# Routed experts 1 to 7 in 64-token tiles of plain 32-bit floats

## The chip, the core and the metric

The kernel runs on one core of a Trainium2 chip. The core has a matrix engine (TensorE, PE in the profile), two engines for elementwise work (VectorE, DVE; ScalarE, ACT), GpSimd (POOL), which here only issues indirect DMAs, and SyncE (SP), which issues the other DMAs. The metric is the device time of one execution in microseconds; a lower time is better.

## The reference

Three stages, all in 32-bit floats. Attention over a window of 128 positions, a dense layer with squared ReLU, and eight routed experts; the change lies in the third.

```python
x = attention(q, k, v)                      # 4 x 8 heads x 576 x 64 -> 2304 tokens x 512
r = maximum(x @ w_in, 0); x = (s * r * r + b) @ w_out          # 512 -> 2048 -> 512
out = x.copy()
do_compute = x @ w_skip > 0;  xc = x[do_compute]
logits = xc @ w_gate;  e_idx = argmax(logits);  gate_w = softmax(logits)[e_idx]
for e in range(8):
    mask = e_idx == e
    h = maximum(xc[mask] @ w1[e], 0.0)                         # 512 -> 1024
    y[mask] = gate_w[mask, None] * (h @ w2[e])                 # 1024 -> 512
out[do_compute] = xc + y
```

For the input given, the routing sends 639, 194, 63, 83, 51, 20, 167 and 143 tokens to experts 0 to 7; 944 tokens of the 2304 skip.

## The kernel before

Tokens are worked on in six blocks of 384 (NB). Attention of a later block is woven between the dense layer's products of an earlier one. Matrix products are made in a fast 32-bit form of PE (F32R) whose inputs are split in a high and a low part (tiles wh and wl, xh and xl): three products, high by high, high by low, low by high, stand for one. The attention's own products (scores s_ps, line 132, and PV o_ps, lines 223 and 253) and all transposes use plain 32-bit floats, unsplit. The PV products of a pair of heads have 64 output columns each and write two halves of PSUM's partitions.

The routing (`route`) of each block writes the numbers of an expert's tokens to a list in DRAM (`lst`), and the dense layer's result goes to DRAM (`x2d`, and `out` for the tokens that skip). In the last block (j = NB - 1) one weight piece of the experts per step m is split (`split`): an expert's weights are 8 pieces of 128 x 1024 (512 KB), each split by one ACT copy (L617) and one DVE subtraction (L68) into wh and wl. Raw pieces arrive in a ring of 5 places, later 12 (`pump`, `Stream`).

`moe2` works through the experts in tiles of 128 tokens. A tile is gathered by an indirect DMA of POOL (xg, L741) by the list in `la`; transposed by PE into p_x (L747) and split into xth and xtl; multiplied with w1 (`gemm1`, 24 products of 512 columns, L755); the ReLU'd result is transposed (`h_t`, 8 transposes, L778) and split; multiplied with w2 (`gemm2`, 24 products, L765); weighted and added by DVE (`fin`, L769) and scattered by POOL (L772). One `step` holds the first products of tile t, the second products of tile t - 1, and between the two halves of these the transposes of tile t + 1. The number of tiles of an expert is known only at run time: `chain` is a tree of branches, one per tile, and `hint` tells PE ahead which way the next one goes. Within the experts ACT, DVE and POOL run in the order in which the code is written; PE's and SP's order, and all that stands ahead of it, is a scheduler's.

```python
            step((e, k), e, prev2, 8 * e + 12, k % 2, 2 if e == 0 else 0, (e, k + 1))
            chain(e, k + 1, e)
```

The lines of these functions as the profile numbers them:

Of the kernel before, what the change touches and what calls it, by code (L numbers as in the profile page):

```python
# [25 lines left out]
KMAX = 6  # L26
BIG = 1 << 20
LE = 128 * 32
RING, MORE = 5, 7
# [4 lines left out]
def body(tc, q_in, k_in, vl, wm, we, wg, wgt, s_in, b_in, mask_in, cst_in, rout_in, ids_in, out):  # L34
# [613 lines left out]
    for j in range(NB):  # L648
        if j:
            split_x(j)  # L650
        if j == NB - 1:
            ast.close()
            R = mk("moe2", ast, side="right", reuse_waits="tile")
            ws.free.extend(R.tile([128, 1024], F32, name=f"ring{i}") for i in range(RING))
            pump()
            later = moe2(tc, locals_ns(locals())).send
# [7 lines left out]
        for m in range(NM):  # L664
# [35 lines left out]
class Stream:  # L700


    def __init__(self):
        self.loaded, self.split, self.places, self.free, self.at = 0, 0, RING, [], {}

    def state(self):
        return self.loaded, self.split, self.places, list(self.free), dict(self.at)

    def back_to(self, st):
        self.loaded, self.split, self.places, self.free, self.at = *st[:3], list(st[3]), dict(st[4])  # L710


# [5 lines left out]
def moe2(tc, L):  # L718
    nc = tc.nc
    main, psum, lst, x2d, out = L.main, L.psum, L.lst, L.x2d, L.out  # L720
    cnt, rc, ident, eh, el, split, ws = L.cnt, L.rc, L.ident, L.eh, L.el, L.split, L.ws
    C = L.R
    xg = [C.tile([128, DM], F32, name=f"xg{i}") for i in range(3)]
    lt = [C.tile([128, 2], U32, name=f"lt{i}") for i in range(3)]
    ls = [C.tile([128, 2], U32, name=f"ls{i}") for i in range(4)]
    la = C.tile([128, NE, NTILE, 2], U32, name="la")
# [7 lines left out]
    extra = []  # L734
    bank = lambda tag, name, bufs=1: psum.tile([128, 512], F32, name=name, tag=tag, bufs=bufs)

    def gather(e, k, rows=NT):
        if (e, k) != (0, 1):
            nc.vector.tensor_copy(lt[0], la[:, e, k, :])
        idx = la[:, e, k, 0:1] if isinstance(k, int) and (e, k) != (0, 1) else lt[0][:, 0:1]  # L740
        nc.gpsimd.indirect_dma_start(  # L741
            out=xg[0], out_offset=None, in_=x2d[0:rows], in_offset=bass.IndirectOffsetOnAxis(ap=idx, axis=0),
            bounds_check=rows - 1, oob_is_err=False)

    def x_t():
        for k in range(4):
            nc.tensor.transpose(p_x[:, k * 128:(k + 1) * 128], xg[0][:, k * 128:(k + 1) * 128], ident)  # L747
# [20 lines left out]
    def fin(n):  # L768
        nc.vector.scalar_tensor_tensor(out=og, in0=p_o, scalar=lt[2][:, 1:2].bitcast(F32), in1=xg[2],  # L769
                                       op0=ALU.mult, op1=ALU.add)  # L770
        nc.vector.tensor_copy(ls[n], lt[2])
        nc.gpsimd.indirect_dma_start(  # L772
            out=out, out_offset=bass.IndirectOffsetOnAxis(ap=ls[n][:, 0:1], axis=0), in_=og, in_offset=None,
            bounds_check=NT - 1, oob_is_err=False)
# [207 lines left out]
```

## Time and profile before

| | us |
|---|---|
| median of 3 timed runs | 802.49 (799.76 to 802.6) |
| profiled execution | 804.8 |
| its span, first to last instruction | 803.0 |
| expert 1's first tile begins on PE (in the span) | 646.98 |
| last second product ends | about 795.6 |

The profile's page gives busy time per engine and 40 equal slices of the span (each 20 us; a digit is tenths). Other views give busy time in chosen stretches, the instructions in order of time (a row may stand for several like ones: the count stands behind the x, the time is from the first's start to the last's end), and for a tile how long its DMAs took from issue to landing. A PE record's end is modelled, so records overlap; what an operation costs PE is the distance between starts. "128*64 128x128" is a product with 128 contraction rows, 64 output columns of the stationary operand, and a moving operand of 128 columns.

### The profile page before, as it was taken

The page shows a single profiled execution, that of the slowest core. Times are in us where ns is not written, and L with a number is a line of the kernel's source. Part 1 is how long each engine was busy: PE and PEld are TensorE (multiplying, and loading weights), DVE is VectorE, ACT ScalarE, POOL GpSimd, SP SyncE. Part 2 cuts the span into 40 slices and gives each one's busy share as a digit, 9 for nine tenths or more (in the row PEclk, how much of TensorE's full clock was granted, in tenths as well). Part 3 has the DMA queues.
Part 4 walks back from the last instruction along what each step waited for, and adds up shares of the span by engine and source line. Part 5 has one row for each costly group of instructions (what it writes and reads, how often), then busy time and mean ns, then how long its engine had stood idle before and what let it go on. Part 6 is the DMA issues. An engine that isn't in the chain of part 4 may idle for free.

```text
span 803.0 us, 12461 instructions
## 1 busy us (share of the span) xinstructions
PE 748.8 (93%) x4166; PEld 614.1 (76%) x4166; DVE 542.5 (68%) x1655; ACT 374.4 (47%) x871; POOL 52.9 (7%) x56
## 2 busy tenths in 40 slices
PE   7889889989999999979999999999999999878996
PEld 4568767768788888868888888989877877666784
DVE  5889999885358954686547972699642264878651
ACT  4656555534455444535555332545522245557440
POOL 0000000000010001000001010000121111111110
PEclk9879999999999999999999999999999999999999
DMA  8945341532105310432112250354443341877100
GB/s 247 319 152 186 119 155 36 181 99 67 54 17 162 89 37 24 145 103 71 35 47 101 79 171 1 124 167 142 135 149 131 133 142 66 307 254 285 38 23 15
DMA packets 50609, 96.53 MB, mean 120 GB/s; under 512 B 8555, under 2 KB 25963, under 8 KB 50497
## 3 DMA queue, kind: packets, MB, share of 16 engines
q1 hardware_dynamic: 45600, 85.82, 33.6%
q0 software_dynamic: 2976, 5.59, 2.2%
q10 hardware_dynamic: 1920, 3.80, 1.4%
q8 instruction: 49, 0.80, 0.4%
q14 instruction: 64, 0.52, 0.2%
HBM read 83.83 MB, written 13.65 MB: 121 GB/s over the span
## 4 chain that ended last, share of the span: by engine, by line
PE 56%; DMA 16%; DVE 15%; issue 8%; ACT 2%; SPq 1%; another core or an unknown queue 0%; POOL 0%; POOLq 0%; DVEq 0%; ACTq 0%
PE acc L126 20%; PE h_ps L126 20%; DMA out<-og,ls 8%; DMA xg<-x2d,la 5%; PE s_ps L126 3%; PE o_ps L126 3%; PE t_ps L126 3%; DVE wl L68 3%; PE p_o L765 2%; DMA hp<-wgt 2%; DVE hp L373 2%; DVE hp L375 2%; PE p_h L755 2%; DVE tp L168 1%; DVE tp L155 1%
## 5 line engine op out<-in xcount | busy, mean ns | idle before, releaser
L126 PE MATMUL h_ps<-xh,wh 128*128 128x384 f32 x380 | 133.9, 352 | 1.3 <-ACT wh L378 1.3
L126 PE MATMUL h_ps<-xh,wl 128*128 128x384 f32 x380 | 129.5, 341 | 3.4 <-DVE wl L68 3.4
L126 PE MATMUL h_ps<-xl,wh 128*128 128x384 f32 x380 | 128.8, 339 | 0.0
L436 ACT ACTIVATE r<-h_ps 128x384 f32<-128x384 f32 x96 | 47.0, 490 | 113.1 <-PE h_ps L126 87.5
L497 DVE CUSTOM_DVE_ANT_0 junk<-x,hp 128x512 bf16<-128x512 f32 x135 | 92.6, 686 | 9.3 <-DMA hp<-wgt 7.8
L437 DVE SCALAR_TENSOR_TENSOR r<-r,sb 128x384 f32<-128x384 f32 x96 | 58.9, 614 | 57.4 <-ACT r L436 57.1
L163 ACT ACTIVATE tp<-tp,stat 128x256 f32<-128x256 f32 (+2 forms) x160 | 74.6, 468 | 41.3 <-DVE stat L155 40.8
L126 PE MATMUL acc<-wh,gh 128*128 128x512 f32 x288 | 86.9, 409 | 0.7 <-ACT gh L446 0.7
L126 PE MATMUL acc<-wh,gl 128*128 128x512 f32 x288 | 84.1, 400 | 0.1
L126 PE MATMUL acc<-wl,gh 128*128 128x512 f32 x288 | 83.0, 396 | 0.0
L446 ACT ACTIVATE gh<-r,sb 128x384 fp32r<-128x384 f32 x96 | 59.2, 617 | 47.0 <-DVE r L437 46.5
L126 PEld LDWEIGHTS h_ps<-xh,wh 128*128 128x128 f32 x380 | 72.1, 190 | 10.4 <-issue 3.8
L155 DVE CUSTOM_DVE_ANT_0 tp<-s_ps,masks 128x256 f32<-128x256 f32 (+2 forms) x160 | 52.6, 378 | 35.1 <-PE s_ps L126 27.2
L126 PEld LDWEIGHTS h_ps<-xh,wl 128*128 128x128 f32 x380 | 72.0, 190 | 5.4 <-DVE wl L68 5.3
L447 DVE SCALAR_TENSOR_TENSOR gl<-r,sb,gh 128x384 fp32r<-128x384 f32 x96 | 59.1, 616 | 22.4 <-ACT gh L446 21.7
L126 PEld LDWEIGHTS h_ps<-xl,wh 128*128 128x128 f32 x380 | 72.2, 190 | 2.0
L126 PEld LDWEIGHTS acc<-wh,gl 128*128 128x128 f32 x288 | 54.2, 190 | 14.6 <-DVE gl L447 1.9
L126 PEld LDWEIGHTS acc<-wl,gh 128*128 128x128 f32 x288 | 54.4, 189 | 12.7
L126 PEld LDWEIGHTS acc<-wh,gh 128*128 128x128 f32 x288 | 50.1, 189 | 10.2 <-issue 3.4
L755 PE MATMUL p_h<-wh,xth 128*128 128x512 f32 x120 | 49.5, 412 | 6.7 <-ACT wh L617 4.4
L591 POOL DMA_INDIRECT lst<-pay,di x18 | 18.9, 1049 | 538.4 <-DVE di L589 534.5
L126 PE MATMUL t_ps<-cst,tp 128*128 128x128 f32 (+1 forms) x246 | 37.2, 271 | 14.5 <-DVE tp L168 13.1
(131 smaller groups left out, 1275.4 us busy)
## 6 DMA issues: line engine op xcount, KB each, us to landing
ring<-we SPq DMA_DIRECT2D x36, 512.0 KB, 4.1
w_words<-wm SPq DMA_DIRECT2D x30, 512.0 KB, 4.7
hp<-wgt SPq DMA_DIRECT2D x45, 256.0 KB, 3.2
more<-we SPq DMA_DIRECT2D x21, 512.0 KB, 5.5
vt<-vl SPq DMA_DIRECT2D x32, 192.0 KB, 2.6
x2d<-x SPq DMA_DIRECT2D x17, 256.0 KB, 2.6
out<-x SPq DMA_DIRECT2D x17, 256.0 KB, 3.0
more<-we ACTq DMA_DIRECT2D x7, 512.0 KB, 3.5
```

The costliest lines, as they stand in the source:

```text
L68: nc.vector.tensor_tensor(out=out_, in0=x, in1=hi.bitcast(F32), op=ALU.subtract)
L126: i = f(*args, **kw)
L155: anchor['v'] = nc.vector.tensor_tensor_reduce(out=t[0:nr, i, c0:c0 + n], in0=ps[i][0:nr, c0:c0 + n], in1=masks[0:nr, 2 * units[u][1] + i, ...
L163: anchor['s'] = nc.scalar.activation(out=t[0:nr, i, c0:c0 + n], in_=t[0:nr, i, c0:c0 + n], func=ACTF.Exp, scale=-1.0, bias=st[0:nr, 0, i:i ...
L373: nc.vector.scalar_tensor_tensor(out=bits, in0=hi, scalar=0xC0000000, in1=bits, op0=ALU.bitwise_and, op1=ALU.bitwise_or)
L436: nc.scalar.activation(out=r, in_=hp, func=ACTF.Relu)
L437: nc.vector.scalar_tensor_tensor(out=r, in0=r, scalar=sb[:, 0:1], in1=r, op0=ALU.mult, op1=ALU.mult)
L446: nc.scalar.activation(out=gh, in_=r, func=ACTF.Identity, bias=sb[:, 1:2])
L447: nc.vector.scalar_tensor_tensor(out=gl, in0=r, scalar=sb[:, 1:2], in1=gh.bitcast(F32), op0=ALU.add, op1=ALU.subtract)
L497: nc.vector.tensor_tensor_reduce(out=junk, in0=x2t[j, t], in1=w, scale=1.0, scalar=0.0, op0=ALU.mult, op1=ALU.add, accum_out=lgs[j][:, t, ...
L591: i = nc.gpsimd.indirect_dma_start(out=lst, out_offset=bass.IndirectOffsetOnAxis(ap=di[:, t:t + 1], axis=0), in_=pay[:, t, :], in_offset=N ...
L755: nc.tensor.matmul(p_h[f], lhsT=x[:, k * 128:(k + 1) * 128], rhs=w[:, f * 512:(f + 1) * 512], start=n == 0, stop=n == 11)
```

## The change

Expert 0 keeps its tiles of 128, its split weights and its steps (`step0`, `chain0`, `leave0`). For experts 1 to 7:

- A tile has 64 tokens. A token's row of 512 is two rows of 256 (`x2h`), so a gather brings 128 half rows: the first halves of 64 tokens on partitions 0 to 63, the second halves on 64 to 127. The list is kept in that layout (`l2`, four loads, then a shift and an or by DVE).
- Products are in plain 32-bit floats, with unsplit weights. The 64 tokens are the stationary operand; the output columns are split in two halves, which go to PSUM partitions 0 to 63 and 64 to 127 (`tile_position`). Per tile 8 calls of 512 columns, 16 calls of 256, and 6 transposes.
- Raw weights lie in 42 places: 3 of the ring, 16 that held split weights 8 to 15 of the dense layer (one pair free after each step of the last block), 7 of the pool `more`, 16 that held expert 0's split weights. The last 14 of the 56 pieces reuse places of expert 1 and what follows.
- The gather of a tile is issued one step earlier than before, into one of four buffers of half the width.
- The last dense block splits 8 pieces, not 16.

```diff
+NQ = 2
+TT = 128 // NQ
+TMAX = 6
 BIG = 1 << 20
 LE = 128 * 32
-RING, MORE = 5, 7
+RING, MORE = 3, 7
+NP = 16 + RING + MORE + 16
...
-    eh, el = {}, {}
-    ws = Stream()
-
-    def pump(eng=nc.sync):
-        while ws.free and ws.loaded < 8 * NE:
-            t, i = divmod(ws.loaded, 8)
-            ws.at[ws.loaded] = ws.free.pop(0)
-            eng.dma_start(out=ws.at[ws.loaded], in_=we[t, i])
-            ws.loaded += 1
-
-    def split(t, i):
-        n = 8 * t + i
-        p = t % 2
-        if (p, i) not in eh:
-            eh[p, i] = W(8 * p + i, "wh")
-            el[p, i] = W(8 * p + i, "wl")
-        raw = ws.at.pop(n)
-        nc.scalar.copy(eh[p, i], raw)
-        lower(el[p, i], raw, eh[p, i])
-        ws.free.append(raw)
-        ws.split = n + 1
-        pump()
...
+    eh, el, raws, pools = {}, {}, {}, {}
+
+    def at_place(n):
+        if n >= NP:
+            return raws[n - NP]
+        if n < RING:
+            return pools["ring"].tile([128, 1024], F32, name=f"ring{n}", tag=f"ring{n}")
+        n -= RING
+        if n < 16:
+            name = f"{('wh', 'wl')[n % 2]}{8 + n // 2}"
+            return main.tile([128, 1024], F32, name="raw", tag=name)
+        n -= 16
+        if n < MORE:
+            return pools["more"].tile([128, 1024], F32, name=f"more{n}", tag=f"more{n}")
+        n -= MORE
+        return main.tile([128, 1024], F32, name="raw", tag=f"{('wh', 'wl')[n % 2]}{n // 2}")
+
+    def fetch(a, b):
+
+        for n in range(a, min(b, 8 * (NE - 1))):
+            raws[n] = at_place(n)
+            nc.sync.dma_start(out=raws[n], in_=we[1 + n // 8, n % 8])
...
+    def fetch0(i):
+
+        if i < 8:
+            spl[i] = pools["ring"].tile([128, 1024], F32, name=f"ring{i % RING}", tag=f"ring{i % RING}")
+            nc.sync.dma_start(out=spl[i], in_=we[0, i])
+
+    def split(i):
+        raw = spl.pop(i)
+        eh[0, i], el[0, i] = W(i, "wh"), W(i, "wl")
+        nc.scalar.copy(eh[0, i], raw)
+        lower(el[0, i], raw, eh[0, i])
...
-            if j == NB - 1:
-                split(*divmod(m, 8))
+            if j == NB - 1 and m < 8:
+                split(m)
+                fetch0(m + RING)
+            elif j == NB - 1:
+
+                if m == 8:
+                    fetch(0, RING)
+                else:
+                    fetch(RING + 2 * (m - 9), RING + 2 * (m - 8))
     last = g2(NB - 1, NM - 1)
+    fetch(RING + 14, RING + 16)
...
+    x2h = x2d.rearrange("n (h d) -> (n h) d", h=NQ)
+    outh = out.rearrange("n (h d) -> (n h) d", h=NQ)
+    xt, ht = xf[0:2]
...
+    def step0(at, second):
+
+
+        if second:
+            shift(1)
+        shift(0)
+        if at is not None:
+            nc.vector.tensor_copy(lf[0], la[:, at, :])
+            rows(xf[0], x2d, lf[0][:, 0:1], NT)
+        gemm1(0, 0)
+        gemm1(0, 1)
+        if second:
+            gemm2(0, 0)
+            if at is not None:
+                x_t(xf[0])
...
+    def leave0():
+        step0(None, True)
+        shift(1)
+        sx_t(here(1, 0))
+        gemm2(0, 0)
+        gemm2(0, 1)
+        fin(3)
+        fetch(NP - 16, NP)
...
+    def sx_t(x):
+        for k in range(XK):
+            nc.tensor.transpose(p_x[:, k * 128:(k + 1) * 128], x[:, k * 128:(k + 1) * 128], ident)
+        nc.vector.tensor_copy(xt[:, 0:HD], p_x[:, 0:HD])
+
+    def sgemm1(e):
+        for k in range(4):
+            for f in range(NQ):
+                nc.tensor.matmul(p_h[0][TT * f:TT * f + TT, 0:HF], lhsT=xt[:, part(k, XK)],
+                                 rhs=w(e, k)[:, f * HF:(f + 1) * HF], start=k == 0, stop=k == 3,
+                                 tile_position=(0, TT * f))
+        nc.scalar.activation(out=r[:, 0:HF], in_=p_h[0][:, 0:HF], func=ACTF.Relu)
+
+    def sgemm2(e, cs):
+        for c in cs:
+            o = (c % 2) * 512
+            for f in range(NQ):
+                nc.tensor.matmul(p_o[TT * f:TT * f + TT, 0:HD], lhsT=ht[:, part(c, HK)],
+                                 rhs=w(e, 4 + c // 2)[:, o + f * HD:o + (f + 1) * HD], start=c == 0, stop=c == 7,
+                                 tile_position=(0, TT * f))
...
+    def sh_t():
+        for c in range(HK):
+            nc.tensor.transpose(p_t[0][:, c * 128:(c + 1) * 128], r[:, c * 128:(c + 1) * 128], ident)
+        nc.scalar.copy(ht[:, 0:HF], p_t[0][:, 0:HF])
...
+    def step(x, cur, e1, e2, n=0, then=None, pre=(), new=None):
+
+
         if e2 is not None:
...
+            second()
+        nc.vector.tensor_copy(xg[0][:, 0:HD], cur[0])
+        nc.vector.tensor_copy(xg[0][:, HD:HD + 2].bitcast(U32), cur[1])
...
+        for p in pre:
+            gather(*p)
+        sgemm1(e1)
+        if then:
+            hint(*then)
+        if e2 is not None:
+            sgemm2(e2, range(4))
+        if x is not None:
+            sx_t(x)
+        if e2 is not None:
+            sgemm2(e2, range(4, 8))
+            sfin(n)
+        sh_t()
...
+            pre = [(e + 1, 1)] + ([(e + 2, 0)] if e + 2 < NE else [])
+            step(here(e + 1, 0), cur, e, prev2, 2 + e % 2, (e + 1, 1), pre)
+            if e > 1:
+                fetch(NP + 8 * (e - 2), NP + 8 * (e - 1))
...
+        fetch(NP - 16 - MORE, NP - 16)
...
-        step((0, 1), None, None, 16)
-        nc.scalar.dma_start(out=la[:, 1:NE], in_=lv[:, 1:NE, 0:NTILE])
-        _, K = nc.values_load_multi_w_load_instructions(ki[0:1, :], min_val=0, max_val=NTILE - 1)
-        K = [k + 1 for k in K]
+        x_t(xf[0])
+        for i in range(NQ):
+            for q in range(NQ):
+                nc.scalar.dma_start(out=l2[TT * q:TT * q + TT, :, i], in_=lv[TT * i:TT * i + TT, 1:NE, 0:NTILE])
...
+            for q in range(NQ):
+                s = slice(TT * q, TT * q + TT)
+                nc.vector.tensor_scalar(out=l2[s, :, :, :, 0], in0=l2[s, :, :, :, 0], scalar1=NQ // 2, scalar2=q,
+                                        op0=ALU.logical_shift_left, op1=ALU.bitwise_or)
+            for p in ((1, 0), (1, 1), (2, 0)):
+                gather(*p)
+
+            step0(2, False)
+            chain0(3)
+            leave0()
+            for e in range(1, NE):
+                chain(e, 1, e - 1 if e > 1 else None, (here(e, 0), meta(e, 0)))
```

On POOL, at the start of the experts (`xg` and `xf` hold a 128-token tile of expert 0, `xn` the 64-token tiles of experts 1 to 7, `ki` the tile counts, `l` the list `l2`), before:

```order
L741 DMA xg_6019<-x2d,lt_6022 128x512
L591 DMA lst<-pay,di 32768x2 x3
L772 DMA out<-og,ls_6026 2304x512
L909 TENSOR_LOAD ki
L852 REGISTER_ALU
L852 COMPARE_AND_BRANCH
L741 DMA xg_6019<-x2d,la 128x512
```

and now:

```order
L774 DMA xf_6017<-x2d,lf_6020 128x512
L596 DMA lst<-pay,di 32768x2 x3
L779 DMA out<-og,ls_6028 2304x512
L1040 TENSOR_LOAD ki
L1041 TENSOR_LOAD ki
L774 DMA xn<-x2d,l_6032 128x256 x3
L774 DMA xf_6017<-x2d,lf_6020 128x512
```

Three gathers for experts 1 and 2 now stand ahead of the gather of expert 0's third tile.

On SP, the same place (`la` is the list of expert 0, `more` are weight places), before:

```order
L475 DMA x2d<-x_6246 128x512
L476 DMA out<-x_6246 128x512
L909 TENSOR_LOAD ki
L909 ISA x16
L901 DMA la<-lst 128x32
L852 REGISTER_ALU
L852 COMPARE_AND_BRANCH
```

and now:

```order
L1041 ISA x10
L1028 DMA la<-lst 128x32
L628 DMA more_6444<-we 128x1024
L628 DMA more_6446<-we 128x1024
L628 DMA more_6448<-we 128x1024
L628 DMA more_6450<-we 128x1024
L628 DMA more_6452<-we 128x1024
L628 DMA more_6454<-we 128x1024
L628 DMA more_6456<-we 128x1024
```

Seven weight loads stand right behind the list of expert 0. Before, the loads into `more` came later, some of them on ACT's queue.

On PE, the end of a step before (the last of the 12 products behind the hint, the transposes of h, the branch, the first products of the next tile):

```order
L765 MATMUL p_o<-wh_5847,hth 128x512
L765 MATMUL p_o<-wl_5848,hth 128x512
L765 MATMUL p_o<-wh_5847,htl 128x512
L778 MATMUL p_t_6354<-cst,r_6033 128x128 x4
L778 MATMUL p_t_6355<-cst,r_6033 128x128 x4
L852 COMPARE_AND_BRANCH
L755 MATMUL p_h_6250<-wh_5549,xth 128x512
```

and a whole step of experts 1 to 7 now (`raw` and `ring` are unsplit weights):

```order
L972 COMPARE_AND_BRANCH
L892 MATMUL p_h_6252<-ring_5887,xf_6017 64x512 x2
L892 MATMUL p_h_6252<-ring_5889,xf_6017 64x512 x2
L892 MATMUL p_h_6252<-ring_5891,xf_6017 64x512 x2
L892 MATMUL p_h_6252<-raw,xf_6017 64x512 x2
L919 ISA
L1121 BRANCH_PREFETCH_HINT
L901 MATMUL p_o<-raw,xf_6018 64x256 x8
L886 MATMUL p_x<-cst,xn 128x128 x2
L901 MATMUL p_o<-raw,xf_6018 64x256 x8
L913 MATMUL p_t_6356<-cst,r_6036 128x128 x4
L972 COMPARE_AND_BRANCH
```

The hint moved from behind the transposes of x to a place ahead of all second products.

## Rows read from the trace of the kernel before

**Rows 1.** The page: busy time and share of the span, DMA by slices.
```profile
PE 748.8 (93%) x4166; PEld 614.1 (76%) x4166; DVE 542.5 (68%) x1655; ACT 374.4 (47%) x871; POOL 52.9 (7%) x56
...
DMA  8945341532105310432112250354443341877100
```
**Rows 2.** Busy time by stretch: length, engines (count), granted clock, DMA share, GB/s.
```profile
606.90:646.90 40.00, 39.05 (x190) 31.52 (x187) 12.33 (x32) 10.14 (x19) 5.56 (x6) 1.00 0.36 125
...
686.90:739.00 52.10, 41.86 (x184) 33.20 (x183) 38.97 (x56) 31.24 (x40) 7.03 (x6) 0.93 0.74 267
739.00:795.70 56.70, 55.86 (x260) 44.55 (x259) 29.91 (x56) 22.70 (x33) 8.76 (x8) 1.00 0.15 54
```
**Rows 3.** Timeline, PE, tile starts: start, length, instruction, count [idle before, releaser].
```profile
642.27 0.48 PE L765 MATMUL p_o<-wh,hth 128*128 128x512 f32 x1
...
645.14 1.04 PE L778 MATMUL p_t<-cst,r 128*128 128x128 f32 x8
...
646.98 0.49 PE L755 MATMUL p_h<-wh,xth 128*128 128x512 f32 x1 [0.80 <-ACT hth L781]
...
659.49 0.48 PE L755 MATMUL p_h<-wh,xth 128*128 128x512 f32 x1
```
**Rows 4.** Timeline, PE, one burst of the attention, and two narrow windows in it.
```profile
59.83 0.88 PE L126 MATMUL o_ps<-pt,vt 128*64 128x128 f32 x12
60.63 1.13 PE L126 MATMUL s_ps<-k,q 64*128 64x256 f32 x8
...
61.17 0.38 PE L126 MATMUL s_ps<-k,q 64*128 64x256 f32 x2
...
61.38 0.38 PE L126 MATMUL s_ps<-k,q 64*128 64x256 f32 x2
```
**Rows 5.** Timeline, PE, transposes followed by half-array products.
```profile
388.31 0.60 PE L126 MATMUL t_ps<-cst,tp 128*128 128x128 f32 x4
388.84 1.29 PE L126 MATMUL o_ps<-pt,vt 128*64 128x128 f32 x14
```
**Rows 6.** Timeline, PE, two tile starts in the loaded stage.
```profile
689.80 0.47 PE L755 MATMUL p_h<-wh,xth 128*128 128x512 f32 x1 [2.72 <-ACT wh L617]
...
724.79 0.47 PE L755 MATMUL p_h<-wh,xth 128*128 128x512 f32 x1 [1.69 <-ACT wh L617]
```
**Rows 7.** Start of the experts: POOL, ACT's queue, PE; landing times of la, of xg.
```profile
596.20 1.00 POOL L591 DMA_INDIRECT lst<-pay,di  x1 [0.31 <-issue]
597.50 0.97 POOL L591 DMA_INDIRECT lst<-pay,di  x1 [0.30 <-issue]
...
603.00 1.04 POOL L741 DMA_INDIRECT xg<-x2d,la  x1 [3.17 <-PE p_h L755]
...
599.62 0.43 ACTq L908 DMA_DIRECT2D la<-lst  x1
...
606.36 0.66 PE L747 MATMUL p_x<-cst,xg 128*128 128x128 f32 x4 [1.05 <-DMA xg<-x2d,la]
...
DMA to landing us min/median/max: 1.7/3.2/3.8
...
DMA to landing us min/median/max: 2.9/3.4/5.2
```
**Rows 8.** Timeline, PE, from 717 us.
```profile
717.23 0.66 PE L747 MATMUL p_x<-cst,xg 128*128 128x128 f32 x4 [4.68 <-DMA xg<-x2d,la]
717.64 0.62 PE L765 MATMUL p_o<-wh,hth 128*128 128x512 f32 x1
718.06 0.63 PE L765 MATMUL p_o<-wl,hth 128*128 128x512 f32 x1
...
722.07 1.03 PE L778 MATMUL p_t<-cst,r 128*128 128x128 f32 x8
```
**Rows 9.** Timeline, the last tile's end: PE and DVE.
```profile
788.30 1.03 PE L778 MATMUL p_t<-cst,r 128*128 128x128 f32 x8
...
795.77 0.75 DVE L769 SCALAR_TENSOR_TENSOR og<-p_o,lt,xg 128x512 f32<-128x512 f32 x1 [4.49 <-PE p_o L765]
```

More of the change, by code (lines that the diff above doesn't have):

```diff
@@ L653, in body @@
             R = mk("moe2", ast, side="right", reuse_waits="tile")
-            ws.free.extend(R.tile([128, 1024], F32, name=f"ring{i}") for i in range(RING))
-            pump()
+            pools["ring"] = R
+            for i in range(RING):
+                fetch0(i)
             later = moe2(tc, locals_ns(locals())).send
@@ L833, in leave @@
-    def leave(e, prev2):
+        nc.vector.tensor_copy(lf[a + 1], lf[a])
+        nc.vector.tensor_copy(xf[a + 1], xf[a])
+    def step0(at, second):
[11 more added lines that the diff above has]
+                x_t(xf[0])
+                if isinstance(at, int):
+                    hint(0, at + 1)
+            gemm2(0, 1)
+            fin(at % 2 if isinstance(at, int) else 2)
+        elif at is not None:
+            x_t(xf[0])
+        h_t()
@@ new lines, in meta, with here, gather, part @@
+    def meta(e, t):
+        return l2[:, e - 1, t % NQ, t // NQ, :]
+    def here(e, t):
+        return xm[t % 2] if t else xin[e % 2]
+    def gather(e, t):
+        rows(here(e, t), x2h, meta(e, t)[:, 0:1], NQ * NT)
+    def part(c, n):
+        return slice((c % n) * 128 + (c // n) * TT, (c % n) * 128 + (c // n) * TT + TT)
+    def sx_t(x):
+        for k in range(XK):
+            nc.tensor.transpose(p_x[:, k * 128:(k + 1) * 128], x[:, k * 128:(k + 1) * 128], ident)
+        nc.vector.tensor_copy(xt[:, 0:HD], p_x[:, 0:HD])
@@ new lines, in hint, with second @@
+    def hint(e, t):
+        if e < NE and t < (TMAX if e else KMAX):
+            tc.mark_branch_hint_location(f"tile{e}_{t}", hint=(K[e] if e else K0) > t,
+                                         engines=[mybir.EngineType.PE])
+    def second():
+        nc.vector.tensor_copy(xg[1].bitcast(U32), xg[0].bitcast(U32))
+    def step(x, cur, e1, e2, n=0, then=None, pre=(), new=None):
+        if e2 is not None:
+            second()
+        nc.vector.tensor_copy(xg[0][:, 0:HD], cur[0])
+        nc.vector.tensor_copy(xg[0][:, HD:HD + 2].bitcast(U32), cur[1])
+        if new is not None:
+            nc.vector.tensor_copy(ltd, new)
+            rows(x, x2h, ltd[:, 0:1], NQ * NT)
+        for p in pre:
[3 more added lines that the diff above has]
+            hint(*then)
+        if e2 is not None:
+            sgemm2(e2, range(4))
[5 more added lines that the diff above has]
+        sh_t()
@@ new lines, in chain @@
+    def chain(e, t, prev2, cur):
+        if t == TMAX:
+            x = xm[(t - 1) % 2]
+            nc.vector.tensor_copy(ltd, cur[1])
+            with tc.For_i(t // NQ, K2[e], 1) as k:
+                for i in range(NQ):
+                    step(x, (x, ltd), e, e, i, new=l2[:, e - 1, i, bass.ds(k, 1), :])
+            leave(e, e, (x, ltd))
+            return
+        with tc.If(K[e] > t, preferred_fallthrough_block=True, label=f"tile{e}_{t}") as c:
+            step(here(e, t), cur, e, prev2, t % 2, (e, t + 1), [(e, t + 1)] if t + 1 < TMAX else [])
+            chain(e, t + 1, e, (here(e, t), meta(e, t)))
@@ new lines, in moe2 @@
+    ki = main.tile([1, 2, NE], I32, name="ki")
+    base = rc[0:1, 32:32 + NTILE].unsqueeze(1).to_broadcast([1, NE, NTILE])
+    count = cnt[0:1, :].unsqueeze(2).to_broadcast([1, NE, NTILE])
+    for i in range(NQ):
+        nc.vector.scalar_tensor_tensor(out=kf, in0=count, scalar=-float(i * TT), in1=base, op0=ALU.add, op1=ALU.is_gt)
+        m = 0 if i else 1
+        nc.vector.tensor_reduce(out=kg[:, :, i], in_=kf[:, :, m:NTILE], axis=AX.X, op=ALU.add)
+    nc.vector.tensor_copy(ki[:, 1], kg[:, :, 0])
@@ L902, in moe2 @@
+    nc.vector.tensor_reduce(out=kf[:, :, 0], in_=kg, axis=AX.X, op=ALU.add)
+    nc.vector.tensor_copy(ki[:, 0], kf[:, :, 0])
+    nc.sync.dma_start(out=la[:, 2:], in_=lv[:, 0, 2:NTILE])
     L.mst.close()
     with tc.tile_pool(name="more", bufs=1, reuse_waits="tile") as E:
-        extra.extend(E.tile([128, 1024], F32, name=f"more{i}") for i in range(MORE))
+        L.pools["more"] = E
+        fetch(NP - 16 - MORE, NP - 16)
         hand = tc.manual_schedule(
             engines={mybir.EngineType.Activation, mybir.EngineType.DVE, mybir.EngineType.Pool})
-        step((0, 1), None, None, 16)
```

160 lines of the change are left out of this document (64 added, 96 removed).

## The prediction

> **What bounds the kernel now.** I read the page first, then the busy time by stage, then PE's timeline of the routed experts, because the change touches nothing else. The page says PE 93% busy over the span and shows the DMA engines loaded at the start and again near the end [rows 1]. By stage [rows 2]: from 606.9 to 646.9 us (expert 0) PE is busy 39.05 of 40 us at full clock; from 686.9 to 739 it is busy 41.86 of 52.1, with the granted clock at 0.93 and DMA at 267 GB/s; after 739 it is 55.86 of 56.7 again. So the routed part is bound by PE, but for some 10 us in the stage where weights of 20- to 83-token experts stream in. Two tile starts show what a tile costs: 646.98 and 659.49, so 12.5 us per 128 tokens [rows 3]. Expert 0 has 5 tiles; experts 1 to 7 have 2, 1, 1, 1, 1, 2, 2, so 10. Those ten fill 646.98 to 795.6, 148.6 us; ten times 12.5 and 6 for the last second products are 131, so some 18 us go to waits and to a slow clock.
>
> **The change part by part.**
>
> *Tiles of 64 tokens.* By the counts of tokens, experts 1 to 7 now have 4, 1, 2, 1, 1, 3, 3 tiles: 15. PE's order gives per tile 8 products of 512 columns, 16 of 256, and 6 transposes. What a plain-float product costs in this form the trace shows in the attention. The four calls of a burst of scores (two groups, two heads) leave 8 records, so a call is two records [rows 4]. The PV products have the very form wanted, 128 rows by 64 columns, on two column halves: 12 records of 128 columns in 0.88 us. Transposes, one after another, take 0.60 us for 4 and 1.04 for 8, so 0.11 us apiece and 0.27 for the last to end [rows 3, 5]. By that tail the 12 records start within 0.60 us, 0.055 apart: two at a time, 0.11 a pair, the halves side by side. Pairs of 256 columns start at 61.17 and 61.38, 0.215 apart [rows 4], twice the 128-column pitch; 512 columns I take at 0.43. First products: 4 pairs of calls, 8 pairs of records, 8 x 0.43 = 3.44. Second products: 16 x 0.215 = 3.44. Transposes 6 x 0.11 = 0.65. Sum 7.5 us.
>
> *Changes of form inside a tile.* The transposes use the whole array, the products half-arrays, and PE's order alternates them: four changes of form per tile. Row by row: 4 transposes start at 388.31, the last at 388.64, and the half-array product at 388.84, 0.20 later where 0.11 would do [rows 5]; the first pair after a change also takes 0.16, not 0.11 (the first group of [rows 4]: 0.60 = 0.16 + 4 x 0.11). So 0.145 a change, 0.58 a tile. A tile costs 8.1 us, against 7.5 if the changes were free and 8.4 if each cost what a transpose's tail shows (0.27 in place of 0.20). The Trainium skill, page "TensorEngine Tiling (Array Packing)", section "Tiling Modes", says that switching the tiling mode drains the engine. The trace agrees in kind, but the gap is 0.20 us and not the 0.27 that the last record lasts. With full drains at every change the total below would be some 4 us longer; the sum goes by the rows.
>
> *Weights unsplit.* ACT and DVE lose one big operation each per 512 KB of weights (56 loads). Off the path they are worth nothing; on it they were part of the 18 us (2.72 us before 689.80 and 1.69 before 724.79 end on ACT's copies [rows 6]). I count no separate gain, since the new tile sum starts from PE alone. Weights now run ahead in 42 places: 26 of them before expert 1 starts, 16 in one go when expert 0's last products end. At the 267 GB/s of [rows 2] those 16 (8.4 MB) take 31 us, and their first use is expert 4, seven tiles (57 us) later. Cost nothing; if that cover failed, a 512 KB load would cost 2 us each.
>
> *Gathers a tile ahead.* They hide behind a whole tile: issue about 1.5 us into a step, one POOL issue of 1.0, landing 3.4 (5.2 at most) [rows 7], against 13 us until the transposes that need it. The waits before p_x (4.68 us at 717.23 [rows 8]) go.
>
> *What the change adds before expert 0's third tile.* The lists of experts 1 to 7 now come in four loads on ACT's queue in place of one, DVE shifts them, POOL issues three gathers from them, and only then the gather of expert 0's third tile, which before went first. In before: lists asked for at 599.62, gather at 603.00, p_x at 606.36, PE idle 1.05 us [rows 7]. Now: four issues of 0.43 end at 601.4; landing 3.2 (1.7 to 3.8) gives 604 to 605, three weight loads beside them (SP sends them right behind its own list) may make it 607; I take 605. DVE's two shifts and copies 0.7. POOL's issues stand 1.3 apart (596.20, 597.50), so the fourth starts 3.9 later, at 609.7; landing 3.4 to 5.2, I take 4.2: 613.9, 7.5 us later than 606.36. Ends 5.5 and 11. PE has nothing else queued: it stalls. After such a stall it runs slow: after 4.68 us idle the next 12 products took 4.43 us, 717.64 to 722.07 [rows 8], most of them 0.43 apart, the lower of the clock's two levels (1.2 GHz), where 642.27 to 645.14 took 2.87 [rows 3]. That is 1.6 more. POOL is behind DVE's wait for the lists here, and PE behind POOL.
>
> *End of the dense part.* The eight splits beside its last steps go (a 0.7 us wait before the last products), but the list load and first gather now share the queues with two weight loads per step, and the first transposes stand 0.7 us earlier in PE's order. I take +0.5 (-0.7 to +2.5).
>
> *The sum.* Before, the transposes of expert 0's last tile start at 645.14 [rows 3]. Now: -0.4 (no x transposes in that step), +0.5, +7.5, +1.6: 654.3. From there to the end of expert 0's second products 7.3 (as 788.30 to 795.6, 0.2 ahead of DVE's 795.77 [rows 9]): 661.6. First 64-token tile, with nothing to fill the wait for ReLU: 5.2. Thirteen at 8.1: 105.4. One without x transposes 7.6. The last second products, with the wait for their transposed input: 4.4. That gives 784.2. Steps end in branches; at ten of them before, PE lost 0 to 2.72 us, 0.80 at 646.98 where no load was late [rows 3, 6]; I add 2 for the fourteen (0 to 8): 786.2. Then the end: 795.6 to 803.0, less 0.3 for half the columns in DVE's last operation (0.75) [rows 9]: 7.1, span 793.3. The profiled execution of before took 804.8, 1.8 above its span, and the median of its three timed runs is 802.49, 2.3 lower. 793.3 + 1.8 - 2.3 = 792.8; I say 793. Its own range is 784 to 800: changes of form at 0.09 (-3), a stall of 5.5 without the slow stretch (-3.6), no branch loss (-2) to the low side; a stall of 11 and the dense part's +2.5 to the high side.
>
> **The rivals.**
>
> *The list loads starve (no change).* The lists are 1792 pieces of 144 bytes, and SP puts seven 512 KB weight loads beside them. If the lists only land when the weights have, that is 3.7 MB at 267 GB/s, 13.7 us: lists at 614, 9 us later, total 802. For it: gathers landed in 5.2 instead of 3.4 us at worst, in a loaded stretch. Against: four of the seven loads stand behind waits for others, and ACT's list is asked first. The Trainium skill, page "DMA: Bandwidth & Descriptors", section "Queues, rings and completion order", says an engine takes turns between queues packet by packet, which would hold small pieces behind large ones; no row here shows lists beside weights. Chance 0.14.
>
> *Branches (slower).* Tiles are shorter, so each of the 14 step changes in experts 1 to 7 has less work in PE's queue to cover the fetch of what follows. If each loses 1.3 us, between that 0.80 and the 1.69 to 2.72 of [rows 6], the total is 793 - 2 + 18 = 809. It decides "slower" from 1.1 us a change. For it: weights stream during the first four tiles, and the dearest changes before were in the loaded stage. Against: those two came where the gather had held back the hint, and most changes cost nothing. Chance 0.15.
>
> *The halves run in turn (slower).* Then a tile costs 6.9 more: 15 x 6.9 = 103, total 896. Only if 512- or 256-column products differ from the 128-column ones of [rows 4]. Chance 0.03.
>
> *Less is added (faster).* If POOL's gathers and the stall cost their low ends and form changes hide: 784. Chance 0.08.
>
> **How the numbers follow.** The forecast has 0.60. What this kernel's measurement can tell from no change is about 0.5%: 798.5 to 806.5. Of the forecast's 0.60, 0.07 lies above 798.5. Faster: 0.53 + 0.08 = 0.61. Same: 0.07 + 0.13 + 0.03 = 0.23. Slower: 0.12 + 0.03 + 0.01 = 0.16. The range runs from 784 to 807: it leaves out the halves in turn, most of the branch rival and little of the low side.
>
> **What would show it.** Right: half-array pairs of 512 columns 0.43 us apart; tile starts 8.1 apart in expert 1; PE idle about 7.5 us from 606 on, ended by the gather, with slow products behind it; no wait before p_x in experts 1 to 7. The first rival shows in list loads landing after 612, the second in idle PE of over 1 us behind the transposes of each tile with every input long there. Wrong altogether: pairs 0.86 apart, or DVE or POOL named before PE's products in every tile.

## The result and the profile after

The changed kernel takes 808.33 us in the median of 17 runs, the kernel before 803.76 on the same chip: ratio 1.0058, 95% interval 1.0033 to 1.0083. It is slower by 4.6 us (0.6%), where 793 us was forecast.

The profiled executions must be read from a common point, the end of the dense layer's last product: 580.00 us before, 575.69 after. The stages ahead of it are the same code but for eight splits of weights fewer in the last dense block. The dense layer ends anywhere from 575.2 to 584.0 us in the thirteen profiles of the changed kernel and its variants, so most of these 4.3 us are a matter of the execution. From there to the end of the span it is 223.0 us before and 227.6 after, 4.6 more. The prediction, 793.3 - 580.0, had 213.3 there. So 14.3 us are to be explained. That this 4.6 equals the difference of the medians is partly luck: three variants below whose routed stage is nearly or wholly the same (`more_late`, `refetch_late`, `half_put`) took 225.3, 225.5 and 224.5 us for the stretch, so up to 3 of the 14.3 us belong to this one execution.

The page, as in [rows 1], and the busy time by stretch, as in [rows 2]; first the page:

```profile
PE 739.8 (92%) x4376; PEld 565.9 (70%) x4376; DVE 466.5 (58%) x1595; ACT 310.8 (39%) x795; POOL 69.4 (9%) x74
...
DMA  8955331531215200532013320557735165461000
```

```profile
606.90:646.90 40.00, 29.80 (x130) 23.43 (x131) 11.04 (x31) 7.28 (x13) 8.13 (x8) 0.83 0.23 81
660.00:700.00 40.00, 38.55 (x235) 19.19 (x233) 7.46 (x27) 5.33 (x9) 9.18 (x9) 1.00 0.54 200
700.00:740.00 40.00, 35.46 (x227) 17.02 (x227) 7.22 (x25) 4.73 (x8) 11.72 (x12) 0.96 0.43 154
740.00:780.00 40.00, 40.00 (x266) 19.00 (x262) 7.75 (x29) 5.92 (x10) 11.85 (x12) 1.00 0.09 27
```

PE is full in the routed experts once the weights are in (740 to 780). The loss is in two stretches: expert 0, where PE is busy 29.80 of 40 us at a clock of 0.83 (39.05 before), and 700 to 740.

A 64-token step, PE's timeline (compare [rows 3 to 5]):

```profile
669.27 2.79 PE L892 MATMUL p_h<-ring,xf 128*64 128x512 f32 x12
...
672.75 1.90 PE L901 MATMUL p_o<-raw,xf 128*64 128x256 f32 x16
674.58 0.44 PE L886 MATMUL p_x<-cst,xn 128*128 128x128 f32 x2
674.95 1.95 PE L901 MATMUL p_o<-raw,xf 128*64 128x256 f32 x16
676.83 0.66 PE L913 MATMUL p_t<-cst,r 128*128 128x128 f32 x4
677.41 2.79 PE L892 MATMUL p_h<-ring,xf 128*64 128x512 f32 x12
```

677.41 - 669.27 = 8.14 us, forecast 8.1. The halves run side by side (16 records, 8 pairs, take 3.48 us), so the tiles themselves gave what was worked out.

The start of the experts, all engines (compare [rows 7]); under it the landing times of the lists `l`:

```profile
597.11 0.33 SPq L1028 DMA_DIRECT2D la<-lst  x1
597.12 3.33 ACTq L1038 DMA_DIRECT2D l<-lst  x4
...
597.48 7.01 SPq L628 DMA_DIRECT2D more<-we  x7
...
606.57 0.60 DVE L1047 TENSOR_SCALAR l<-l 64x252 uint32<-64x252 uint32 x2 [9.72 <-DMA l<-lst]
607.97 1.05 POOL L774 DMA_INDIRECT xn<-x2d,l  x1 [10.92 <-DMA more<-we]
...
611.95 1.00 POOL L774 DMA_INDIRECT xf<-x2d,lf  x1 [0.30 <-issue]
...
615.26 1.11 PE L786 MATMUL p_x<-cst,xf 128*128 128x128 f32 x4 [11.21 <-DMA xf<-x2d,lf]
```

```profile
DMA to landing us min/median/max: 2.7/5.3/7.9
```

The lists are asked for at 597.12 and the last is there at 606.5, then the three gathers `xn` go, then that of expert 0's third tile (`xf`, 611.95), and PE stands for 11.21 us. Before, PE stood for 1.05 us here. The next 24 products take 7.69 us, where 24 take 5.85 at full clock.

Expert 2 to expert 3's second tile, POOL's and PE's timelines together, the landing times of `xn` in that stretch, and those of the write-out `out` at 705.68 with who waited for it (compare [rows 8]):

```profile
694.06 1.02 POOL L779 DMA_INDIRECT out<-og,ls  x1 [4.12 <-DVE ls L908]
...
703.05 1.02 POOL L774 DMA_INDIRECT xn<-x2d,l  x1 [7.98 <-PE p_t L913]
...
704.38 1.00 POOL L774 DMA_INDIRECT xn<-x2d,l  x1 [0.30 <-DVE xg L931]
705.68 1.03 POOL L779 DMA_INDIRECT out<-og,ls  x1 [0.30 <-issue]
...
712.90 0.66 PE L886 MATMUL p_x<-cst,xn 128*128 128x128 f32 x2 [4.54 <-DMA out<-og,ls]
...
713.49 3.31 PE L901 MATMUL p_o<-raw,xf 128*64 128x256 f32 x16
```

```profile
DMA to landing us min/median/max: 7.9/8.3/8.6
```

```profile
  PE p_x L886: 4.5, 1
...
DMA to landing us min/median/max: 7.1/7.1/7.1
```

The step starts at 694.83. Its gathers go at 703.05 and 704.38 and land 8.6 and 7.9 us later, at 711.69 and 712.24. The first of them is expert 3's second tile, which PE wanted at 708.36. PE goes on only at 712.90, and its next 16 products take 3.3 us where 1.95 is usual. The row names what ended the wait, and rightly: the write-out of the tile before, issued third, at 705.68. The records of PE's sequencer, which hold its waits and branches, show it step by step. PE waits for semaphores, the counters that tell of a landing: for the gather's until 711.72 and then for the write-out's until 712.80; the write-out landed at 712.77. So 3.3 us of the 4.54 are a late gather and 1.1 a write-out behind it. Why the program has PE wait for a write-out no run shows.

What POOL did from 695.2 to 700.5 no row of a timeline shows: the records of its sequencer have a taken branch there (a jump to another place in the program) and nothing for 5.19 us. Behind it POOL waited until 702.2 for the write-out issued at 694.06, which took 8.1 us to land, and then issued the gather. (The gather's row names PE's transposes p_t; in `gated_first` it went 0.28 us before these had ended, so it does not wait for them.)

The end (compare [rows 9]):

```profile
794.65 0.48 DVE L906 SCALAR_TENSOR_TENSOR og<-p_o,xg 128x256 f32<-128x256 f32 x1 [4.12 <-PE p_o L901]
...
795.47 0.97 POOL L779 DMA_INDIRECT out<-og,ls  x1 [3.99 <-DVE ls L908]
```

From PE's last product to the end it is 8.7 us, 7.3 before: DVE is 0.3 us shorter as forecast, but POOL's closing drain takes 5.38 instead of 3.99 us.

### The profile page after: what moved, and what is told of

Its sections match the earlier page's. It is cut to its first block, busy times and chain, and to the rows that moved or that the text cites. A ratio compares the mean times of both kernels' runs of the same rounds, so it can differ in the third digit from the quotient of the medians.

```text
span 803.3 us, 12832 instructions
## 1 busy us (share of the span) xinstructions
PE 739.8 (92%) x4376; PEld 565.9 (70%) x4376; DVE 466.5 (58%) x1595; ACT 310.8 (39%) x795; POOL 69.4 (9%) x74
## 4 chain that ended last, share of the span: by engine, by line
issue 68%; DMA 22%; PE 4%; POOL 2%; SPq 1%; DVE 1%; POOLq 0%; ACTq 0%; ACT 0%; DVEq 0%
DMA out<-og,ls 14%; DMA xn<-x2d,l 2%; PE p_h L794 2%; POOL lst L596 1%; DMA w_words<-wm 1%; DMA l<-lst 1%; DMA lst<-pay,di 1%; PE p_o L804 1%; DMA xf<-x2d,la 1%; PE acc L131 1%; DMA masks<-mask 1%; DMA lst<-x 1%; SPq L109 0%; DMA xf<-x2d,lf 0%; DMA la<-lst 0%
## 5 line engine op out<-in xcount | busy, mean ns | idle before, releaser
L131 PE MATMUL t_ps<-cst,tp 128*128 128x128 f32 (+1 forms) x246 | 36.0, 265 | 15.1 <-DVE tp L173 13.7
L901 PE MATMUL p_o<-raw,xf 128*64 128x256 f32 x392 | 48.4, 390 | 0.7 <-ACT xf L914 0.7
```

The lines of the kernel that those rows point to most:

```text
L131: i = f(*args, **kw)
L901: nc.tensor.matmul(p_o[TT * f:TT * f + TT, 0:HD], lhsT=ht[:, part(c, HK)], rhs=w(e, 4 + c // 2)[:, o + f * HD:o + (f + 1) * HD], start=c = ...
```

## The experiments

Three theories. Theory 1, for the start: the lists' small pieces starve beside the 512 KB weight loads, and three gathers stand ahead of the one that PE waits for. Theory 2, for the wait at 712.90: the gather is starved by the 14 late weight loads, or issued late by POOL, or both. (The expectations below speak of the gather alone; the write-out behind it was not thought of.) Theory 3 checks a term of the sum that seemed right, the changes of form.

**Loads later in the text** (`more_late`)

```diff
-        fetch(NP - 16 - MORE, NP - 16)
...
             step0(2, False)
+            fetch(NP - 16 - MORE, NP - 16)
```

> Edit: the loads of seven weight pieces into `more` are issued behind expert 0's third tile instead of beside the four loads of the lists. Theory 1 (the small pieces of the lists are served in turn with the 4 KB pieces of the weights): the lists land about 602 instead of 606.5 us, every step behind them on VectorE and GpSimd moves forward with them, and the idle time of TensorE before the transposes of expert 0's third tile falls from 11.2 to about 6.8 us; time 808.3 - 4.4 = about 804, ratio to the kernel before 1.000. Rival (four list loads of their own cost it, or GpSimd's order alone): the lists land at 606 as now, idle time 11 us, ratio 1.006.

Ratio 1.0054 (1.0021 to 1.0086), idle time 12.0 us. The loads still went out from 599.6 us, right behind the list's: SP waits for nothing there and runs ahead of the other engines. The edit moved nothing, so it says nothing on theory 1.

**The gather first** (`gather_first`)

```diff
             rows(xf[0], x2d, lf[0][:, 0:1], NT)
+        if lists:
+            lists()
         gemm1(0, 0)
...
-            step0(2, False)
+            step0(2, False, lists)
```

`lists` is the shift of the lists and the three gathers.

> Edit: the gather of expert 0's third tile stands ahead of the shift of the lists and of the three gathers for experts 1 and 2 on VectorE and GpSimd; all the loads stay. Theory 1 (three gathers and the wait for the lists stand ahead of this one on GpSimd): it is issued about 600 us, when its index has landed, and lands about 603.6 to 607; idle time before its transposes 0 to 3 us instead of 11.2, and the next first products lose their slow clock (1.85 us); time 808.3 - 10 = about 798, ratio 0.992. Rival (the transfers beside it, not the order): the gather itself lands after 8 to 9 us beside the weights, idle time 5 us or more, ratio about 0.999.

Ratio 0.9952 (0.9930 to 0.9975). The profiled execution is the slowest of the ten (807.85 us; their median is 798.66), and its dense layer ended 6.1 us later than that of the changed kernel above. Idle time 3.43 us: the gather went at 606.31 and took 7.0 us to land, beside the weights; 3.3 us in the changed kernel, where it went later. The order on POOL was most of the stall, the transfers the rest.

**The loads held back** (`more_gated`)

```diff
-        fetch(NP - 16, NP)
+        fetch(NP - 16, NP - 15)
+        fetch(NP - 16 - MORE, NP - 16)
+        fetch(NP - 15, NP)
```

The first of these waits for its place, in the profile until 648.5 us. SP is also made to keep the written order, and the earlier fetch of `more` is taken out.

> The first try (the same loads later in the program's text) left SyncE's loads where they were, since SyncE waits for nothing there and runs ahead: it tested nothing. Here the seven loads into `more` stand behind a load that waits for a place in use until about 655 us, so that nothing runs beside the four loads of the lists. Theory 1 (small pieces starve beside 4 KB pieces): the lists land about 602 instead of 606.5 us, the idle time before expert 0's third tile falls from 11.2 to about 6.8 us (three gathers still stand ahead of its own on GpSimd); against the 806.9 of the changed kernel about 802, ratio 1.000. Rival (the order on GpSimd alone): lists at 606, idle time 11 us, ratio 1.005.

The start in its timeline:

```profile
600.31 2.74 ACTq L1040 DMA_DIRECT2D l<-lst  x4
604.66 0.61 DVE L1049 TENSOR_SCALAR l<-l 64x252 uint32<-64x252 uint32 x2 [4.19 <-DMA l<-lst]
...
606.06 1.05 POOL L774 DMA_INDIRECT xn<-x2d,l  x1 [5.39 <-DVE lf L832]
...
610.03 1.00 POOL L774 DMA_INDIRECT xf<-x2d,lf  x1 [0.30 <-issue]
...
613.54 1.11 PE L786 MATMUL p_x<-cst,xf 128*128 128x128 f32 x4 [6.21 <-DMA xf<-x2d,lf]
```

From the first issue to DVE 4.3 us instead of 9.4, idle time 6.21 instead of 11.21. Theory 1 holds in the profile: 5.0 of the 11.2 us are lists starved beside weights. The Trainium skill, "DMA: Bandwidth & Descriptors", section "Queues, rings and completion order", has the engines take turns between queues by packets; these two numbers agree with it. The ratio, 1.0037 (1.0010 to 1.0064), fell by less than the 5 us; the intervals are too wide to tell a gain of 4 us from none.

**Both** (`gated_first`)

> Both edits: expert 0's third gather first, and the `more` loads held back. With the gather first alone 3.4 us of idle time stayed, its gather landing 6.7 us after its issue at 606.3 beside the weights. Theory 1: now the gather lands in 3.3 us, before TensorE needs it: idle time under 0.5 us, time about 798.7 - 3 = 795.5, ratio 0.991. Rival (the gather is late for its index, not for the weights): idle time stays above 2.5 us, ratio 0.995.

POOL and PE in its timeline:

```profile
604.62 1.05 POOL L774 DMA_INDIRECT xf<-x2d,lf  x1 [3.12 <-PE p_h L794]
...
607.03 1.01 POOL L774 DMA_INDIRECT xn<-x2d,l  x1 [1.36 <-DVE l L1052]
...
608.02 0.66 PE L786 MATMUL p_x<-cst,xf 128*128 128x128 f32 x4 [0.82 <-DMA xf<-x2d,lf]
...
693.84 1.03 POOL L774 DMA_INDIRECT xn<-x2d,l  x1 [7.77 <-PE p_o L905]
...
696.47 1.02 POOL L779 DMA_INDIRECT out<-og,ls  x1 [0.30 <-issue]
...
703.05 0.41 PE L890 MATMUL p_x<-cst,xn 128*128 128x128 f32 x2 [3.62 <-DMA out<-og,ls]
```

The gather lands in 3.4 us, the idle time is 0.82 us, the ratio 0.9881 (0.9824 to 0.9937), by the ratios 5.7 us better than with the gather first alone. The start stall was these two things but for the 0.82 us.

The last three rows are the wait of theory 2 in this run. The gather issued at 693.84 landed at 699.41, just before PE wanted the tile (699.43); the 3.62 us are the write-out alone, which landed at 702.91. In `more_late`, `pair` and `half_put` too the gather was there in time and PE stood 2.57, 1.39 and 2.99 us for the write-out. In all nine profiles that have this wait PE's sequencer goes on within 0.04 us of the write-out's landing.

**The last 14 loads later** (`refetch_late`, then `places`)

```diff
-            if e > 1:
-                fetch(NP + 8 * (e - 2), NP + 8 * (e - 1))
+            if e > 2:
+                fetch(NP + 8 * (e - 3), NP + 8 * (e - 2))
```

> Edit: the 14 pieces that take the places of used ones are fetched one expert later (8 at the end of expert 3, 6 at the end of expert 4). Theory 2 (the 4.5 us wait before expert 3's second tile is a gather that lands after 8.6 us beside 4 MB of weights): this gather lands in about 3 us, the idle 4.5 us and the 1.4 us of slow clock behind it go: 808.3 - 5.9 = about 802.4, ratio 0.998; a part may come back before a tile of expert 5, where the loads now fall. Rival (GpSimd issued the gather late because its instructions came late): the gather is issued at 703 as now and the wait stays at 3 us or more; ratio 1.004 to 1.006.

Again SP ran ahead: 12 of the 14 loads went out as before, the last two at 722.5 and 723.4 instead of 707.5 and 708.4. Wait 4.01 us, ratio 1.0047 (1.0011 to 1.0083). It tested nothing. So the places were changed too, and with them the time at which a load can start:

```diff
-            return raws[n - NP]
+            return raws[n - NP + 16]
```

> The 14 last pieces take the places of expert 3 and 4 instead of those of expert 1 and 2, so that their loads cannot start before about 721 us (moving the loads in the text had moved only two of them). Theory 2 (the 4.5 us wait before expert 3's second tile is a gather starved beside these loads): the gather issued about 703 lands in 3 to 4 us, the wait and the slow clock behind it go: about 806.9 - 5.5 = 801.4, ratio 0.998; a wait of 1 to 3 us may arise where expert 6's weights come late. Rival (GpSimd fetches its instructions for 5 us behind the taken branch and issues the gather 8 us late): idle time of 2 us or more stays, ratio 1.003 to 1.005.

Landing times of `xn` from 690 to 712 us (three gathers), and PE's waits behind them:

```profile
DMA to landing us min/median/max: 2.6/2.7/4.0
```

```profile
719.55 1.94 PE L892 MATMUL p_h<-more,xf 128*64 128x512 f32 x8 [1.02 <-issue]
...
733.48 5.35 PE L892 MATMUL p_h<-raw,xf 128*64 128x512 f32 x16 [4.61 <-issue]
```

The two gathers of this step land in 2.6 and 2.7 us instead of 8.6 and 7.9, the write-out behind them in 2.1 instead of 7.1, and nothing waits at expert 3's second tile. POOL's taken branch is quicker as well, 2.77 us instead of 5.19, so the gather goes at 698.84. The slowness moved with the loads, now issued from 711.5 to 724.4: a write-out of 718.81 takes 6.9 us, and POOL's next taken branch 4.78 where it took 2.53. They meet another branch too: PE's own, out of expert 4, takes 5.95 us in its sequencer's records where it took 0.52, and PE stands 4.61 us. Ratio 1.0123 (1.0061 to 1.0185): worse than with the wait. The Trainium skill, "Runtime: NRT & Kernel Launch", section "Instruction fetch mechanics", says that a taken branch whose target isn't at hand fetches it by DMA; the branches here that grow with the weight traffic (POOL's 2.77 and 4.78 us) agree.

**Gathers an expert ahead** (`ahead`)

```diff
-xn = C.tile([128, 4, HD], F32, name="xn")
+xn = C.tile([128, 5, HD], F32, name="xn")
...
-            pre = [(e + 1, 1)] + ([(e + 2, 0)] if e + 2 < NE else [])
+            pre = [(e + 2, 0), (e + 2, 1)] if e + 2 < NE else []
```

> An expert's second tile is gathered one expert ahead, as its first is now, into a fifth place of the tile buffer; loads stay as they are. One more gather stands on GpSimd at the start, behind that of expert 0's third tile in need but ahead of it in order: the start stall grows by 1.3 us. Theory 2 in either form (starved gather or late GpSimd) expects the 4.5 us wait and the 1.4 us of slow clock gone: 806.9 - 5.9 + 1.3 = about 802.3, ratio 0.999. Rival (TensorE's own instructions come late behind its branches there): a wait at the same place stays, ratio 1.006.

The 4.54 us wait is gone, the start stall is 13.15 us (1.9 more, 1.3 expected), and 1.63 us of idle time stands one tile earlier. The row names "issue" as its end, but PE's sequencer stands there until 705.08 for a write-out issued at 697.48, which landed at 705.05: again a write-out. Ratio 1.0020 (0.9985 to 1.0055), a gain that the intervals do not tell from none.

**A hint for POOL** (`pool_hint`)

```diff
-                                         engines=[mybir.EngineType.PE])
+                                         engines=[mybir.EngineType.PE, mybir.EngineType.Pool])
```

> The changed kernel, with the hint of the next branch's direction given to GpSimd as well as to TensorE; nothing else moves. Theory 2 as it now stands (two halves: GpSimd's instructions come 5.3 us late behind the taken branch at 695, so that the gather is issued 8 us into the step, and then its pieces are starved for 8.6 us): with the instructions there, the gather is issued at about 698, lands before 708.4, and the 4.5 us wait falls below 1 us: about 806.9 - 5 = 802, ratio 0.9985. Rival (starving alone, whenever it is issued): the wait stays above 3 us, ratio 1.005.

The expectation failed: two branches of POOL now cost 5.06 and 3.50 us in a row, the gather goes at 706.63, the wait grows to 5.98 us, ratio 1.0104 (1.0045 to 1.0163). The hint did not bring the instructions in time, so the run does not decide between the theory and its rival. It agrees with the late half of theory 2: the gather and the write-out behind it, both issued 3.6 us later, made PE wait 1.4 us longer. Nor could the branch alone have brought the gather to 698: the write-out for which POOL waits behind it landed only at 703.06.

**The changes of form** (`pair`)

```diff
             sgemm2(e2, range(4), hr)
-        if x is not None:
-            sx_t(x)
+        last = sh_t(hw)
+        if x is not None:
+            with tc.issue_after(last.ins):
+                last = sx_t(x)
         if e2 is not None:
-            sgemm2(e2, range(4, 8))
+            with tc.issue_after(last.ins):
+                sgemm2(e2, range(4, 8), hr)
             sfin(n)
-        sh_t()
```

> Edit: in each 64-token step the transposes of the hidden layer stand directly before those of the next tile, in the middle of the second product, and the transposed hidden layer has three places in turn; so TensorE changes between 128x64 and 128x128 form twice a step instead of four times, and does not wait for the copy of the hidden layer. Theory 3 (a change costs 0.145 us, as worked out before): 14 steps x 2 x 0.145 = 4.1 us less, and the 0.7 us before the last product: a step takes 7.85 instead of 8.15 us, time about 803.5, ratio 1.000. Rival (a change costs nothing, the time is in the transposes): a step stays at 8.1 us, ratio 1.005.

PE's timeline:

```profile
680.23 2.74 PE L895 MATMUL p_h<-ring,xf 128*64 128x512 f32 x12
...
688.07 2.75 PE L895 MATMUL p_h<-ring,xf 128*64 128x512 f32 x12
...
699.99 2.83 PE L895 MATMUL p_h<-raw,xf 128*64 128x512 f32 x6 [3.90 <-DMA ring<-we]
```

The step takes 7.84 us, 0.30 less for two changes of form fewer: 0.15 each, as worked out. But the kernel takes 815.17 us, ratio 1.0171 (1.0152 to 1.0191). In the changed kernel the hidden layer's transposes were the last work of a step, and PE's sequencer reached the branch 2.4 us before the next step's first product where nothing waits; now 1.8 us before. Four branches out of an expert show: 5.19, 3.37, 3.91 and 3.50 us in the sequencer's records (2.93, 0.43, 0.52 and 0.88 in the changed kernel), 3.90, 2.09, 2.25 and 1.98 us of PE's idle time, and slow products behind three of them. (The row names a load as the end of the first wait; the branch is over 0.17 us before.) Why these branches also took longer is open: weights stream beside the first (321 GB/s), but not beside the others (10, 40 and 5); so the run shows the price of a change of form, and of branches with less cover, together.

**The end** (`half_put`)

```diff
-            sfin(3)
+            sfin(3, TT)
```

> The changed kernel, with its very last write-out cut to the first 64 partitions, so that columns 256 to 511 of the last 15 tokens stay unwritten: a probe of the end, where GpSimd drains for 5.38 us behind that write-out (3.99 us in the kernel before), the same in every trace to 0.01 us. Theory (the drain grows with the rows written: 30 half rows now, 15 whole rows before, 1.39 us for 15): with 15 half rows 3.99 us. Rival 1 (it grows with the 128 entries of the index): about 2.7 us. Rival 2 (fixed by the program, not by this write-out): 5.38 us.

5.38 us, as in the changed kernel: neither the rows nor the entries of that write-out set it. What does is open.

**The version to keep** (`first_ahead`, `all_three`)

> Expert 0's third gather first, the `more` loads held back, and an expert's second tile gathered one expert ahead. The start stall stays under 1 us. At expert 3's second tile nothing waits; where the step before it waited 1.6 us for GpSimd's late bookkeeping behind the branch, that stays. Against 793.8 of the first two edits: 3.6 + 2.0 + 1.7 of slow clock - 1.6 = 5.7 us less, about 788, ratio 0.981. Rival (the wait only moves to another tile of experts 2 to 7): 793, ratio 0.988.

789.1 us, ratio 0.9819 (0.9760 to 0.9877): faster than both kernels. Its stretch from 700 to 740 us, as above:

```profile
700.00:740.00 40.00, 40.00 (x268) 19.14 (x266) 8.17 (x30) 5.92 (x10) 13.35 (x13) 1.00 0.27 93
```

From the end of the dense layer to the end it is 207.9 us, 15.1 less than before. The one wait left of note is 1.57 us, with "issue" as its end in the row. As in `ahead`, PE's sequencer stands there for a write-out, until 691.21 us; it was issued at 683.52 and landed at 691.17.

> The three edits and GpSimd's branch hint. If the 1.6 us wait left by the gathers an expert ahead is GpSimd's branch, it goes: about 786.5, ratio 0.979. Rival (that wait is a transfer): as without the hint, 788, ratio 0.981.

792.8 us, ratio 0.9858 (0.9800 to 0.9917): in time the two kernels can't be told apart. The wait itself is the rival's, a transfer. It shrank to 0.21 us in this profile because the same write-out landed in 6.5 us instead of 7.7, not because of POOL's branch, which still took 4.39 us (5.63 without the hint).

## Why the prediction was wrong

Of the 14.3 us, measured from the end of the dense layer:

- *Expert 0's third tile, +5.2.* Its transposes were forecast 34.4 us after the dense layer's end and came 39.6 after. The step that failed is the landing of the lists: "I take 605" allowed 5.4 us from the first list's issue, and it took 9.4, since their pieces waited beside weights (4.3 without them). The first rival had the mechanism with a higher price, lists that land only with the last weight. POOL's three gathers (3.98 us for 3.9) and the gather itself (3.3 for 4.2) were sized right or better; DVE's shifts and copies up to the first gather took 1.4 for 0.7. Another 1.55 us came from ahead of the lists, where 12 products from 582 us took 4.59 instead of 3.04 at a granted clock of 0.63; seven of the thirteen profiles of the changed kernel and its variants have that (4.37 to 4.59), six do not, and the one profile before does not (3.03): it comes and goes between executions, and whether it does so without the change is open.
- *From there to expert 1, +1.8.* The slow stretch after the stall was 1.85 us for 1.6, and the first products at 645 took 6.48 us for 5.85; the other 0.9 us is spread.
- *Experts 1 to 7, +5.7.* Forecast 124.6 us, measured 130.3. The tile was right: 8.14 us for 8.1. The miss is one wait, 4.54 us and some 1.4 of slow clock behind it. The step that failed is "they hide behind a whole tile: issue about 1.5 us into a step": the gather went 8.2 us into it, behind a taken branch of POOL and a write-out, and landed in 8.6 us, not 3.4 to 5.2. That made it 3.3 us late; the write-out issued behind it ended the wait 1.1 us later, and the sum had no term for write-outs at all. Their common cause is the late loads: with these moved away (`places`) branch, gathers and write-outs are quick and the wait is gone, and at that run's 2.6 and 2.1 us of landing even issues at 703.05 and 705.68 would have been in time for 708.36. With it failed "cost nothing" for the weights: I asked whether PE waits for them, not what waits beside them. The size of the wait is this execution's: it was 2.57 to 3.95 us in five other profiles whose edits leave this stage alone (`more_late`, `gather_first`, `more_gated`, `gated_first`, `half_put`).
- *The second rival, branches.* They cost PE 1.06 us in all in this profile, half of the 2 allowed, so the rival's 1.3 us at each of 14 did not come. But in `gather_first` and `gated_first`, whose edits lie well ahead of it, the branch right behind the wait took 5.80 and 5.94 us and PE stood 2.26 and 1.98 us for it. Single branches can cost what the rival said.
- *The end, +1.6.* POOL's closing drain, 1.39 us longer, was not in the sum.

The edits of `gated_first` and `ahead` together (`first_ahead`) give back 19.7 us by the profiles (227.6 - 207.9), more than the miss, because the stall that I had accepted in the forecast is gone as well.

## What to carry to other kernels

A weight prefetch that PE never waits for still has a price: while it ran here, index lists, gathers, write-outs and the instructions behind a taken branch each took about twice as long or more, and whichever of them PE waited for next became the bound. Hold such loads behind a wait that ends when the small transfers are through; moving their call in the text does nothing on a queue that runs ahead. Put the transfer that the matrix engine needs first also first on its issuing engine, and issue gathers far enough ahead to cover a late issue and a slow landing at once. When a row names a releaser that makes no sense, such as a write-out ahead of a transpose, compare the landing with the end of the wait before putting another cause in its place.

## What the hardware showed that was not expected

Beside the late weight loads (364 GB/s from 703.0 to 712.8 us in the changed kernel) the gather of expert 3's second tile landed in 5.6 to 8.6 us in seven profiles and the write-out behind it in 6.1 to 7.1; in `places`, with the loads moved away, in 2.6 and 2.1. POOL's branch there took 5.19 us (2.77 in `places`), PE's branch out of expert 4 in `places` 5.95 us (0.52). Idle time of nearly one length had PE's next products at either clock level. In `pair`, after 1.98 us idle, 16 products took 5.35 us (granted clock 0.68, most of them at the lower level), and after 2.09 us 3.65 (1.00); ahead of both PE had run 3.7 us and more without a pause at full clock. POOL's closing drain was 5.37 to 5.38 us in every trace of the changed kernel and its variants, whatever was written last, and 3.99 in the kernel before.
